# W1's first quarter in two loads: four partitions ahead of everything, the other 124 in the old place

## The chip, the cores and the metric

The kernel runs on one core of one Trainium2 chip. The metric is the device time of one execution in microseconds. Before the change, three executions took 302.37, 302.70 and 302.79 us, a median of 302.7.

## What is computed

Two stages, the second fed by the first. The first is attention with a sliding window: 8 batches, 8 heads, 576 positions, 64 features a head; each position sees the 32 positions on either side of it. The second takes the result as 4608 tokens of 512 features, multiplies it with `w_in` (512 x 2048), takes the square of the positive part, and multiplies with `w_out` (2048 x 512).

```python
scores = scale * np.matmul(q, k.transpose(0, 1, 3, 2))
mask = np.abs(pos[:, None] - pos[None, :]) <= window      # window = 32
...
attn = attn / (np.sum(attn, axis=-1, keepdims=True) + 1e-09)
...
x = np.ascontiguousarray(attn_out.transpose(0, 2, 1, 3)).reshape(B * S, H * D)
h = x @ w_in
r = np.maximum(h, 0.0)
return ((r * r) @ w_out)
```

## The kernel before

The tokens are worked off in 24 groups of 192, three to a batch. For a group, Q and K come into SBUF with positions on the partitions and are turned, so that features lie on the partitions: for the first two batches by TensorE (`turn_pe`, L455 to L500), later by DMA transposes (`turn_dma`, L502). `scores` (L517) multiplies two windows of 128 keys with their queries (L548), ScalarE takes the exponential, VectorE multiplies with the mask (in group 0 a bias does that, L531), and `pv` (L581) multiplies with V, which has a column of ones beside it for the sums (L605). VectorE divides; the result is turned once more (`xturn`, L635) into `XT`, features on partitions, the operand of the second stage.

There `mm1` (L708) multiplies `XT` with 128 columns of W1 at a time, four matmuls that add up over the 512 features (L720). ScalarE takes the positive part (L726), VectorE squares it (L729), and `mm2` (L733) multiplies with W2, four of its sixteen slices at a time (L740).

W1 stands in SBUF as 128 partitions x 4 x 2048 in bf16; in HBM it is float32. It is loaded in four quarters of 512 columns: `load_w1` (L437) issues one DMA a quarter from GpSimd, 128 partitions with 4 rows of 512 elements each, which changes the type on the way. `mm1` waits for the quarter that holds its columns. W2 is loaded in four quarters likewise (L442).

The order of the work is a planner's. Every operation is recorded with its engine, what it reads and writes, a key and an estimated duration; a DMA also has an estimated number of moves and the time of one (`move`). `schedule` (L115) lets each engine take the ready operation with the lowest key, with a model of the DMA queues in it, and `emit` (L220) writes every engine's operations in the planned order, with waits on semaphores: one per engine and one per kind of DMA. Within an engine the order is fixed from then on.

Loads at the start follow a list written by hand, OPENING (L59): entry n gets the key -100 + n. It begins with K of group 1, W1's first quarter, V of groups 0 and 1, Q of group 1. Those are all GpSimd DMAs. Q and K of group 0 do not go through GpSimd but come from SyncE (`load_hw`, L381). Where TensorE would have nothing to do in the first 40 us of the plan, `schedule` puts matmuls on zeros (L207 to L217, issued at L310), called fillers below.

```python
OPENING = [("k", 1), ("w1", 0), ("v", 0, 0), ("v", 1, 1), ("q", 1), ("v", 0, 1), ("q", 2), ("k", 2), ("v", 1, 0), ("w1", 1),
```

Of the kernel before, what the change touches and what calls it, by code (L numbers as in the profile page):

```python
# [18 lines left out]
RING = 1536  # L19
NV, NRAW = 6, 6  # L20
NTURN = 2
NXT = 3
LEAD = 13.0
LAG = 9.0
AHEAD = 9.0
FAR, GFAR = 9.0, 99
TISS = 1340
TMOVE = 15
NVR = 24
# [2 lines left out]
XSLACK = 2500  # L32
LSLACK = 5000
# [5 lines left out]
NPR = 3  # L39
# [5 lines left out]
XTD = 1  # L45
# [222 lines left out]
class Gen:  # L268
# [100 lines left out]
    def load_qk(self, t, b, g, key):  # L369
        t0, n = KC[g] if t == "k" else (192 * g, 192)  # L370
        h = n // 2
        G = 3 * b + g
        raw = self.RAW[t][G % NRAW]
        src = (self.q if t == "q" else self.k)[b]
        s = src[:, t0:t0 + n, :].rearrange("h (j p) d -> p j h d", j=2)
        for j in range(2):
            self.p.rec("POOL", lambda e, j=j: e.dma_start(raw[0:h, j, :].rearrange("p (h d) -> p h d", h=8), s[:, j]),  # L377
                       writes=[("raw", t, G % NRAW, j)], dma=(f"{t}{G % NRAW}{j}", G), key=key, dur=500 + 3 * h,
                       move=(h // 2, 14.5), name=f"{t}{b}{g}{j}", after=self.moe if b > 1 else None, slack=LSLACK if b > 1 else 0)

    def load_hw(self, t, g, key):  # L381

        t0, n = KC[g] if t == "k" else (192 * g, 192)
        h = n // 2
        raw = self.RAW[t][g % NRAW]
        u = 2 * (t == "q")
        f = self.OEB[:, u:u + 2, :].rearrange("p a c -> p (a c)")
        s = (self.q if t == "q" else self.k)[0][:, t0:t0 + n, :].rearrange("h (p r) d -> p h (r d)", r=2)
        oe = [("oe", u), ("oe", u + 1)]
        self.p.rec(HWQ[t], lambda e: e.dma_start(f[0:h, :].rearrange("p (h c) -> p h c", c=128), s), writes=oe,  # L390
                   dma=(f"h{u}", g), key=key, dur=420, move=(h // 2, 27), name=f"h{t}{g}")
        for r in range(2):
            x = f[0:h, :].rearrange("p (h r d) -> p h r d", r=2, d=64)[:, :, r, :]
            y = raw[0:h, r, :].rearrange("p (h d) -> p h d", d=64)
            w = [("raw", t, g % NRAW, r)]
            if HWC[t][r] == "ACT":
                self.p.rec("ACT", lambda e, x=x, y=y: e.activation(y, x, ACTF.Copy), reads=oe, writes=w, key=key, dur=600,
                           name=f"c{t}{g}{r}")
            else:
                self.p.rec("DVE", lambda e, x=x, y=y: e.tensor_copy(y, x), reads=oe, writes=w, key=key, dur=430, name=f"c{t}{g}{r}")  # L400

    def load_pair(self, t, b, g, key):

        t0, n = KC[g] if t == "k" else (192 * g, 192)
        h = n // 2
        G = 3 * b + g
        pr, raw = self.PR[t][G % NPR], self.RAW[t][G % NRAW]
        s = (self.q if t == "q" else self.k)[b][:, t0:t0 + n, :].rearrange("h (p r) d -> p h (r d)", r=2)
        self.p.rec("POOL", lambda e: e.dma_start(pr[0:h, :].rearrange("p (h c) -> p h c", c=128), s), writes=[("pr", t, G % NPR)],  # L409
                   dma=(f"{t}p{G % NPR}", G), key=key, dur=500 + 3 * h, move=(h // 2, 20), name=f"{t}{b}{g}",  # L410
                   slack=LSLACK1 if b else 0)
        self.p.rec("DVE", lambda e: e.tensor_copy(raw[0:h, :, :].rearrange("p r (h d) -> p r h d", d=64),
                                                  pr[0:h, :].rearrange("p (h r d) -> p r h d", r=2, d=64)),
                   reads=[("pr", t, G % NPR)], writes=[("raw", t, G % NRAW, x) for x in range(2)], key=3 * G - LEAD - PKEY if b == 0 else key, dur=430,
                   name=f"c{t}{b}{g}")

    def load_v(self, b, g, key, js=(0, 1)):
        G = 3 * b + g
        vt = self.V[G % NV]
        for j in js:  # L420
            k0 = 192 * g - 32 + 128 * j
            lo, hi = max(k0, 0), min(k0 + 128, S_)
            if g and j == 0 and G < NVR:
                lo = k0 + 64
            n = hi - lo
            self.p.rec("POOL", lambda e, j=j, lo=lo, hi=hi, k0=k0: e.dma_start(  # L426
                vt[lo - k0:hi - k0, j, :, 0:64], self.v[b, :, lo:hi, :].rearrange("h p d -> p h d")),
                writes=[("v", G % NV, j)], dma=(f"v{G % NV}{j}", G), key=key, dur=500 + 3 * n, move=(n // 2, 14.5),
                name=f"v{b}{g}{j}", after=self.moe if b > 1 else None, slack=LSLACK if b > 1 else LSLACK1 * b)

    def copy_v(self, G, key):
# [4 lines left out]

    def load_w1(self, d, key):  # L437
        src = self.w_in[:, 512 * d:512 * d + 512].rearrange("(f p) c -> p f c", p=128)
        self.p.rec("POOL", lambda e: e.dma_start(self.W1[:, :, 512 * d:512 * d + 512], src),  # L439
                   writes=[("w1", d)], dma=(f"w1{d}", 0), key=key, dur=770, move=(32, 81), name=f"w1{d}")  # L440

    def load_w2(self, d, key):  # L442
        src = self.w_out[512 * d:512 * d + 512, :].rearrange("(k p) c -> p k c", p=128)
        self.p.rec("POOL", lambda e: e.dma_start(self.W2[:, 4 * d:4 * d + 4, :], src),
                   writes=[("w2", d)], dma=(f"w2{d}", 0), key=key, dur=770, move=(32, 81), name=f"w2{d}")

# [186 lines left out]
    def xturn(self, G):  # L635
        xa, xb = self.XA[G % 3], self.XB[G % 3]
        key = 3 * G - LEAD + 0.5
        r = 192 * G % RING
        wr = [("xt", (3 * G + c) % (RING // 64)) for c in range(3)]
        if G < NXT:  # L640
# [3 lines left out]
            if two and XTD:  # L644
# [7 lines left out]
                def fa(e):  # L652
                    for j in range(4):
# [6 lines left out]
                           name=f"XT{G}0")  # L660
                for x in (1, 2):
# [3 lines left out]
                    src = hts[x // 2][:, 0:256].rearrange("p (j q) -> p j q", j=2)  # L665
                    w = [(t, x) for t in wr[1:]]
                    if x == 1:
                        self.p.rec("ACT", lambda e, dst=dst, src=src: e.activation(dst, src, ACTF.Copy), reads=tag, writes=w, key=key,
                                   dur=act(256), name=f"XT{G}1")
                    else:  # L670
                        self.p.rec("DVE", lambda e, dst=dst, src=src: e.tensor_copy(dst, src), reads=tag, writes=w + wr[1:], key=key,
                                   dur=dve(256), name=f"XT{G}2")
# [16 lines left out]
            if two:  # L689
                for x, (c0, c1) in enumerate(((0, 64), (64, 192))):  # L690
                    self.p.rec("ACT", lambda e, x=x, c0=c0, c1=c1: e.activation(
                        self.XT[:, :, r + c0:r + c1], (ps, pb)[x][:, 0:768].rearrange("p (j q) -> p j q", j=4)[:, :, c0:c1], ACTF.Copy),
                        reads=(bank, bank2)[x], writes=(wr[:1], wr[1:])[x], key=key - 0.01 * (1 - x), dur=act(4 * (c1 - c0)),
                        name=f"XT{G}{x}")
# [3 lines left out]
                       reads=bank, writes=wr, key=key, dur=act(768), name=f"XT{G}")  # L698
            return
        self.p.rec("SP", lambda e: e.dma_start(self.XT[:, :, r:r + 64], xa[64:128, :], transpose=True),  # L700
                   reads=[("xa", G % 3)], writes=wr[:1], dma=(f"xa{G % 3}", G), key=key - 0.3, dur=TISS, move=(16, TMOVE), name=f"T{G}a",
                   slack=XSLACK)
        self.p.rec("SP", lambda e: e.dma_start(self.XT[:, :, r + 64:r + 192], xb[:], transpose=True),
                   reads=[("xb", G % 3)], writes=wr[1:], dma=(f"xb{G % 3}", G), key=key, dur=TISS, move=(32, TMOVE), name=f"T{G}b", slack=XSLACK)

    def mm1(self, t0, n, ds, key):  # L708
        k = self.k1
        self.k1 += 1  # L710
        ht, rt, gt = self.HT[k % 2], self.RT[k % 4], self.GT
        r = t0 % RING
        c = n * len(ds)
        d0 = ds[0]
        steps = [(t0 // 64 + x) % (RING // 64) for x in range(n // 64)]

        def f(e):
            for x, d in enumerate(ds):
                for ft in range(4):
                    mm = e.matmul(ht[:, n * x:n * x + n], self.W1[:, ft, 128 * d:128 * d + 128], self.XT[:, ft, r:r + n],  # L720
                                  start=(ft == 0), stop=(ft == 3))
            return mm

        self.moe = self.p.rec("PE", f, reads=[("xt", s) for s in steps] + [(("xt", s), 1) for s in steps if t0 < 192 and XTD] + [("w1", d0 // 4)], writes=[f"ht{k % 2}"], key=key,
                   dur=4 * len(ds) * max(n / 2.4 + 2.5, 33), name=f"A{t0}.{d0}")
        self.p.rec("ACT", lambda e: e.activation(rt[:, 0:c], ht[:, 0:c], ACTF.Relu), reads=[f"ht{k % 2}"],  # L726
                   writes=[("rt", k % 4)], key=key, dur=act(c), name=f"r{t0}.{d0}")
        rr = rt[:, 0:c].rearrange("p (d t) -> p d t", d=len(ds))
        self.p.rec("DVE", lambda e: e.tensor_tensor(gt[:, d0:d0 + len(ds), r:r + n], rr, rr, ALU.mult),  # L729
                   reads=[("rt", k % 4)], writes=[("gt", s, d) for s in steps for d in ds], key=key, dur=dve(c),  # L730
                   name=f"g{t0}.{d0}")
# [50 lines left out]
    def build(self):  # L782
        p = self.p
# [19 lines left out]
        for n, it in enumerate(self.opening()):  # L803
            kd, a = it[0], it[1:]
# [18 lines left out]
        for G in range(NG):  # L823
# [7 lines left out]
                    key = 3 * G - LEAD - 0.5 if G >= VCS else key  # L831
                    at(key + 0.01, self.copy_v, G, key - VKEY if G >= VCS else key)
            for t in "kq":
                key = 3 * G - LEAD - (0.6 if b < NTURN else 3)
                at(key, self.turn_pe if b < NTURN else self.turn_dma, t, b, g, key)
            for ws in ((0,), (1,)) if G < NSPLIT else ((0, 1),):
                at(3 * G - LEAD + 0.3 * ws[0], self.scores, G, ws)
# [58 lines left out]
```

## Time and profile before

| | |
|---|---|
| median of three executions | 302.7 us |
| the profiled execution | 302.49 us |
| its span, first to last instruction | 300.5 us |
| granted TensorE clock | 1.000 on average |
| GpSimd's DMA queue (q0) | 106016 packets, 17.93 MB, 87.3% of 16 engines' span |
| SyncE's DMA queue (q1) | 49264 packets, 12.14 MB, 29.6% |
| W1's four loads | 512 KB each, median 11.1 us from issue to landing |

The profile is of one execution. Its times are counted from the first instruction; an engine's busy time leaves out the issuing of DMAs by SyncE and ScalarE, waits and branches. In lists by line, "out<-in" names the tiles. A DMA has two times: how long GpSimd is busy with its issue, and how long it takes from the issue until its semaphore is complete, which is called landing here. The semaphore of a DMA of GpSimd goes up in sixteen steps, and the trace holds the time of each. The DMA share of a stretch is the time that packets took, over the core's 16 DMA engines; it is over 1.00 where packets overlap.

### The profile page before, as it was taken

To read this page: it belongs to the slowest core of one execution; us is meant where nothing else is said; L and a number is where in the kernel's file an instruction comes from. 1 tells how busy PE (TensorE), PEld (TensorE's weight loads), DVE (VectorE), ACT (ScalarE), POOL (GpSimd) and SP (SyncE) were. 2 spreads that over 40 slices of the span, in tenths; PEclk is the share of its full clock that TensorE was granted. 3 is DMA by queue.
4 is the path that set the end of the run, shared out by engine and by line. 5 is a ranking of instruction groups with operands and counts; after the bars stand their busy time and mean duration, and the time that the engine had idled before them with its cause. 6 is when DMAs were issued, how large, how long until landed. Compare 5 with 4: busy or idle time off the path is not lost.

```text
span 300.5 us, 6217 instructions
## 1 busy us (share of the span) xinstructions
PE 291.3 (97%) x2394; PEld 171.1 (57%) x2431; DVE 165.8 (55%) x385; ACT 160.5 (53%) x250; POOL 107.4 (36%) x143
## 2 busy tenths in 40 slices
PE   6899999999999999999999999999999999999996
PEld 2588866847677777754444445445445444444445
DVE  6997785727776766654577756556456322222100
ACT  3596834827467656553756566645646343443312
POOL 8993336506653553665155555420000000000000
PEclk9999999999999999999999999999999999999999
DMA  9999999999999999999999999996121200100112
GB/s 170 176 205 184 196 178 171 156 209 130 164 138 174 191 136 182 143 166 198 190 141 157 138 157 139 185 183 142 55 59 39 61 35 35 37 35 36 37 70 105
DMA packets 160636, 39.83 MB, mean 133 GB/s; under 512 B 149984, under 2 KB 156128, under 8 KB 160608
## 3 DMA queue, kind: packets, MB, share of 16 engines
q0 software_dynamic: 106016, 17.93, 87.3%
q1 hardware_dynamic: 49264, 12.14, 29.6%
q10 hardware_dynamic: 5328, 9.37, 9.5%
q8 instruction: 19, 0.31, 0.5%
q14 instruction: 9, 0.07, 0.1%
HBM read 36.70 MB, written 9.44 MB: 154 GB/s over the span
## 4 chain that ended last, share of the span: by engine, by line
PE 88%; DMA 7%; POOL 3%; issue 1%; ACT 1%; POOLq 0%; ACTq 0%
PE ht L720 40%; PE outp L740 39%; DMA w<-in_moe_w_in_dram 5%; PE at L605 4%; PE at L548 3%; DMA xt<-xb 2%; POOL v L426 1%; POOL w L439 1%; PE at L468 1%; POOL qpair L409 1%; PE ht L765 1%; PE outp L765 1%; POOL kpair L409 1%; ACT oe L750 0%; ACT rt L726 0%
## 5 line engine op out<-in xcount | busy, mean ns | idle before, releaser
L720 PE MATMUL ht<-xt,w 128*128 128x256 bf16 (+2 forms) x886 | 142.7, 302 | 1.6 <-DMA w<-in_moe_w_in_dram 0.6
L740 PE MATMUL outp<-w,gt 128*128 128x512 bf16 x535 | 134.3, 379 | 1.4 <-issue 0.2
L726 ACT ACTIVATE rt<-ht 128x512 bf16<-128x512 f32 (+1 forms) x152 | 86.5, 578 | 91.5 <-PE ht L720 88.1
L720 PEld LDWEIGHTS ht<-xt,w 128*128 128x128 bf16 x896 | 81.0, 98 | 44.1 <-DMA w<-in_moe_w_in_dram 1.0
L729 DVE TENSOR_TENSOR gt<-rt 128x512 bf16<-128x512 bf16 (+1 forms) x152 | 61.5, 408 | 64.3 <-ACT rt L726 62.9
L740 PEld LDWEIGHTS outp<-w,gt 128*128 128x128 bf16 x560 | 52.1, 98 | 55.5 <-ACT oe L750 1.0
L377 POOL DMA_DIRECT2D kraw<-in_k_dram x36 | 27.8, 780 | 88.7 <-PE at L548 45.1
L572 ACT ACTIVATE e<-at 128x1024 bf16<-128x1024 f32 x46 | 44.9, 1023 | 10.3 <-PE at L548 10.1
L577 DVE TENSOR_TENSOR pt<-e,mask 128x1024 bf16<-128x1024 bf16 x46 | 31.5, 691 | 24.9 <-ACT e L572 24.7
L426 POOL DMA_DIRECT2D v<-in_v_dram x48 | 38.1, 808 | 0.0
L750 ACT ACTIVATE oe<-outp 128x512 f32<-128x512 f32 x35 | 21.1, 603 | 23.9 <-PE outp L740 23.9
L377 POOL DMA_DIRECT2D qraw<-in_q_dram x36 | 27.7, 778 | 0.0
L605 PEld LDWEIGHTS at<-v,pt 128*128 128x128 bf16 x384 | 18.2, 98 | 9.7 <-issue 1.4
L605 PE MATMUL at<-v,pt 128*128 128x65 bf16 x384 | 20.0, 194 | 0.6 <-ACT pt L569 0.5
L627 DVE TENSOR_TENSOR xa<-at,rs 64x512 bf16<-64x512 f32 x24 | 16.7, 695 | 0.9
L627 DVE TENSOR_TENSOR xb<-at,rs 128x512 bf16<-128x512 f32 x24 | 16.6, 691 | 0.9
L624 DVE RECIPROCAL rs<-at 64x8 f32<-64x8 f32 (+1 forms) x48 | 10.0, 209 | 10.4 <-PE at L605 9.1
L548 PEld LDWEIGHTS at<-qt,kt 64*128 64x128 bf16 x384 | 10.8, 94 | 8.5 <-issue 6.8
L548 PE MATMUL at<-qt,kt 64*128 64x128 bf16 x384 | 15.3, 217 | 0.3
L633 DVE MEMSET at<- 64x520 f32 x23 | 11.3, 492 | 3.6 <-DVE xa L627 2.7
L433 DVE COPY v<-v 64x512 bf16<-64x512 bf16 x16 | 5.5, 341 | 7.2 <-PE ht L720 6.0
L772 DVE COPY oe<-ht 128x128 f32<-128x128 f32 x1 | 0.3, 292 | 14.5 <-PE ht L765 14.5
(67 smaller groups left out, 81.6 us busy)
## 6 DMA issues: line engine op xcount, KB each, us to landing
out_dram<-oe ACTq DMA_DIRECT2D x35, 256.0 KB, 4.4
qraw<-in_q_dram POOLq DMA_DIRECT2D x36, 96.0 KB, 5.7
w<-in_moe_w_in_dram POOLq DMA_DIRECT2D x4, 512.0 KB, 11.1
v<-in_v_dram POOLq DMA_DIRECT2D x16, 128.0 KB, 7.8
w<-in_moe_w_out_dram POOLq DMA_DIRECT2D x4, 512.0 KB, 18.5
v<-in_v_dram POOLq DMA_DIRECT2D x16, 96.0 KB, 7.3
kraw<-in_k_dram POOLq DMA_DIRECT2D x12, 112.0 KB, 4.7
kraw<-in_k_dram POOLq DMA_DIRECT2D x12, 96.0 KB, 5.6
```

The costliest lines, as they stand in the source:

```text
L377: self.p.rec("POOL", lambda e, j=j: e.dma_start(raw[0:h, j, :].rearrange("p (h d) -> p h d", h=8), s[:, j]), writes=[("raw", t, G % NRAW, ...
L426: self.p.rec("POOL", lambda e, j=j, lo=lo, hi=hi, k0=k0: e.dma_start(vt[lo - k0:hi - k0, j, :, 0:64], self.v[b, :, lo:hi, :].rearrange("h ...
L548: mm = e.matmul(sc[:, 512 * par + 128 * j:512 * par + 128 * j + 128], kt[r:r + 64, j, k0:k0 + 128], q, start=G >= NBIAS, stop=True, skip_g ...
L572: self.p.rec("ACT", lambda e, e_=e_, sc=sc: e.activation(e_[:], sc, ACTF.Exp, scale=0.125), reads=tags[w], writes=[("e", n % 2)], key=key, ...
L577: self.p.rec("DVE", lambda e, pt=pt, ee=ee, mb=mb: e.tensor_tensor(pt[:], ee, mb, ALU.mult), reads=[("e", n % 2), ("mask", mi)], writes=[( ...
L605: mm = e.matmul(avp[:, c:c + 65], pt[:, 4 * (h % 2) + h // 2, :], vt[:, w, h, 0:65], start=(w == 0 and y == 0), stop=True, skip_group_chec ...
L627: self.p.rec("DVE", lambda e: e.tensor_tensor(x[r0:128, :].rearrange("p (x y c) -> p x y c", x=2, y=4), av[:, :, :, 0:64], rb, ALU.mult), ...
L720: mm = e.matmul(ht[:, n * x:n * x + n], self.W1[:, ft, 128 * d:128 * d + 128], self.XT[:, ft, r:r + n], start=(ft == 0), stop=(ft == 3))
L726: self.p.rec("ACT", lambda e: e.activation(rt[:, 0:c], ht[:, 0:c], ACTF.Relu), reads=[f"ht{k % 2}"], writes=[("rt", k % 4)], key=key, dur= ...
L729: self.p.rec("DVE", lambda e: e.tensor_tensor(gt[:, d0:d0 + len(ds), r:r + n], rr, rr, ALU.mult), reads=[("rt", k % 4)], writes=[("gt", s, ...
L740: mm = e.matmul(op[:], gt[:, d, r:r + 128], self.W2[:, d, :], start=(d == 0), stop=(d == 15))
L750: self.p.rec("ACT", lambda e: e.activation(oe, op[:], ACTF.Copy), reads=[f"outp{u % 2}"], writes=[("oe", u % 4)], key=key, dur=act(512), n ...
```

## The change

`load_w1` issues the first quarter as two DMAs. The first carries partitions 0 to 3 (16 rows of 512 elements). Its key is -100.5, below every other load's key, so it is GpSimd's first DMA. The second carries partitions 4 to 127 (496 rows) and keeps the key that the whole quarter had. The other three quarters stay as they are. Each part has a semaphore of its own, and the products with W1's first 512 columns wait for both. The remaining lines of the diff give names to constants and keep their values.

```diff
+TINY = 4
+FIRSTKEY = -100.5
...
     def load_w1(self, d, key):
         src = self.w_in[:, 512 * d:512 * d + 512].rearrange("(f p) c -> p f c", p=128)
-        self.p.rec("POOL", lambda e: e.dma_start(self.W1[:, :, 512 * d:512 * d + 512], src),
-                   writes=[("w1", d)], dma=(f"w1{d}", 0), key=key, dur=770, move=(32, 81), name=f"w1{d}")
+        for i, (p0, p1) in enumerate(((0, TINY), (TINY, 128)) if d == 0 and TINY else ((0, 128),)):
+            self.p.rec("POOL", lambda e, p0=p0, p1=p1: e.dma_start(self.W1[p0:p1, :, 512 * d:512 * d + 512], src[p0:p1]),
+                       writes=[("w1", d) if p1 == 128 else "w1first"], dma=(f"w1{d}{i}", 0), key=key if p1 == 128 else FIRSTKEY,
+                       dur=770 if p1 == 128 else 400, move=(max((p1 - p0) // 4, 1), WMOVE), name=f"w1{d}" if p1 == 128 else "w1first")
...
-        self.moe = self.p.rec("PE", f, reads=[("xt", s) for s in steps] + ... + [("w1", d0 // 4)], writes=[f"ht{k % 2}"], key=key,
+        self.moe = self.p.rec("PE", f, reads=[("xt", s) for s in steps] + ... + [("w1", d0 // 4)] + ["w1first"] * (d0 < 4 and TINY > 0), writes=[f"ht{k % 2}"], key=key,
```

In the built programs the orders on TensorE, VectorE, ScalarE and SyncE are the same; GpSimd has the four partitions' DMA ahead of K of group 1, and 124 partitions where 128 were:

```
before                                        after
L313 Iota dif 128x128                         L322 Iota dif 128x128
                                              L449 DMACopy w1 4x4x512
L409 DMACopy kpair1 96x8x128                  L418 DMACopy kpair1 96x8x128
L439 DMACopy w1 128x4x512                     L449 DMACopy w1 124x4x512
L426 DMACopy v0 96x8x64                       L435 DMACopy v0 96x8x64
L426 DMACopy v1 128x8x64                      L435 DMACopy v1 128x8x64
L409 DMACopy qpair1 96x8x128                  L418 DMACopy qpair1 96x8x128
```

## The prediction

> **What bounds the kernel now.** I read the page's head and busy times first, then TensorE's waits, then the chain of waits up to 30 us, then the opening's timeline and its loads.
>
> ```profile
> span 300.5 us, 6217 instructions
> ...
> PE 291.3 (97%) x2394; PEld 171.1 (57%) x2431; DVE 165.8 (55%) x385; ACT 160.5 (53%) x250; POOL 107.4 (36%) x143
> ```
>
> TensorE (PE) is busy for 97% of the span: whatever delays the start of its dense work is added to the end. TensorE's waits from 30 us on:
>
> ```profile
> PE ht L720 <- ACT oe L750: 0.3, 2, 0.2
> PE outp L740 <- issue: 0.2, 1, 0.2
> PE ht L720 <- issue: 0.2, 1, 0.2
> ```
>
> After 30 us it waits 0.7 us in all, none of it for a DMA. There is no slack later in which a late start could be made good. So the opening decides; the chain of waits there, in order of time (start, us, what):
>
> ```profile
> 8.21 0.68 POOL v L426
> 8.89 1.47 POOL w L439 x2
> 10.36 13.73 DMA w<-in_moe_w_in_dram
> 24.09 0.05 issue
> 24.14 1.49 PE ht L720 x16
> ```
>
> The last quarter of W1 is issued at 10.36 and lands at 24.09; TensorE starts on it at 24.14. Before it come GpSimd's issues, back to back. TensorE's own timeline of these 24 us (start, us; idle time before it in brackets):
>
> ```profile
> 1.20 2.74 PE L310 MATMUL outp<-zz 128*128 128x512 bf16 x6 [1.20 <-DVE zz L304]
> ...
> 7.87 1.68 PE L310 MATMUL outp<-zz 128*128 128x512 bf16 x7
> ...
> 10.13 0.51 PE L468 MATMUL outp<-ident,kraw 96*128 96x96 bf16 x8
> 11.19 0.41 PE L605 MATMUL at<-v,pt 128*128 128x65 bf16 x8 [0.54 <-ACT pt L569]
> 11.44 1.46 PE L310 MATMUL outp<-zz 128*128 128x512 bf16 x6
> ...
> 17.19 0.83 PE L720 MATMUL ht<-xt,w 128*128 128x192 bf16 x8
> ...
> 24.14 1.49 PE L720 MATMUL ht<-xt,w 128*128 128x192 bf16 x16 [0.59 <-DMA w<-in_moe_w_in_dram]
> ```
>
> The reader is to see four points: the first product with V (11.19), the first use of the changed quarter (17.19), the wait for the last quarter (0.59 us at 24.14), and the fillers of L310, which take 457 ns each at the start and 240 ns later.
>
> When each load lands is its issue plus its time to landing, asked of the trace one load at a time. In the order of issue: K of group 1 at 7.44, **W1's first quarter 2.31 + 7.3 = 9.63**, V at 10.35 and 11.15, Q at 12.22, V 13.07, Q 14.20, K 15.05, V 15.53, W1's other quarters 19.44, 21.33, 24.09. The queue serves its loads in that order without a pause: what one load takes longer, all behind it land later. GpSimd's timeline and the first quarter's landing:
>
> ```profile
> 1.41 0.91 POOL L409 DMA_DIRECT2D kpair<-in_k_dram  x1 [0.34 <-issue]
> 2.31 0.78 POOL L439 DMA_DIRECT2D w<-in_moe_w_in_dram  x1
> 3.07 1.68 POOL L426 DMA_DIRECT2D v<-in_v_dram  x2
> ```
> ```profile
> DMA to landing us min/median/max: 7.3/7.3/7.3
> ```
>
> **The change, part by part.** The order of instructions on PE, DVE, ACT and SP is the same in both kernels, fillers included; the renamed constants keep their values. GpSimd gets one more DMA (4 partitions x 4 rows of 512) ahead of all others, and the quarter's own DMA, still second among the old ones, carries 124 partitions. The first product with W1 waits for one semaphore more.
>
> *The extra issue.* Its price is not in the trace. Loads cost GpSimd 0.69 us (64 partitions of V) to 0.91 us (128); 16 packets instead of 512 should be at or below the lower: 0 to 0.9 us, taken 0.5. All GpSimd issues move by that. The queue covers it: V's issue ends at 3.86 and its data comes only after 9.63, 5.8 us later. Only K of group 1, first in the queue, is uncovered: its packets start at 5.1 us in the trace, 2.8 after its issue ended. If that start moves with its issue, all loads move by 0.5; if it hangs on the queue's first issue, it comes earlier.
>
> *The wait.* The small load is first in the queue; it lands long before the 124 partitions. Nothing is late by it: 0.
>
> *The 124 partitions.* This is the term that decides. The quarter is 128 x 4 = 512 packets of one row of 512 elements. In the trace its sixteen completion steps, one a DMA engine, lie between 9.09 and 9.63: equal shares, 32 packets each. Every load of this queue has 64, 80, 96, 112 or 128 partitions, all multiples of 16, and the sixteen completions of each of the nine loads ahead of W1's second quarter lie within 0.7 us. So sixteen equal shares of whole partitions fit all that the trace shows. 124 partitions have no sixteen equal shares; the largest number up to 16 that divides them is 4. No load of this kind was run, so I bound: from 31 or 32 packets an engine (any uneven split over all sixteen; price 0), over 124 (four engines with 31 partitions each), to 496 on one. I take **four engines with 124 packets**, since equal shares are all that the rows show.
>
> The price of a packet: 32 of them lie between K's landing at 7.44 and the quarter's at 9.63, 68 ns each; from 19.44 to 24.09 two quarters land, 73 ns each. Ends: the 100 ns that a packet is recorded to take if nothing overlaps (1.27 x 16 engines x 2 us / 397 packets in the row below), and 39 ns (68 x 203 / 350) if the 203 GB/s of that row could rise to the 350 GB/s that the finest slices of the opening reach. I take 73, the later of the two measured rows.
>
> ```profile
> 7.00:9.00 2.00, 1.52 (x14) 0.96 (x15) 1.86 (x7) 1.25 (x2) 2.00 (x4) 1.00 1.27 203
> ```
>
> 124 - 32 = 92 packets more on the four engines, x 73 ns = **6.7 us** (3.6 to 9.2). A load lands when its slowest engine is done, so every later load of the queue lands 6.7 us later although twelve engines are ahead.
>
> The Trainium skill (DMA: Bandwidth & Descriptors, on why a DMA increments its semaphore by 16) states the same divisor: the largest count up to 16 that divides both outermost sizes, 100 partitions giving 10. The same place names an exception for some direct copies that GpSimd issues, which use all sixteen engines with a rounded-up share. By the rule the sum is this one, by the exception the second case below; no run here shows either.
>
> *What TensorE does with it.* The product with V needs V's 10.35 + 6.7 = 17.05 instead of starting at 11.19: 5.9 us late, since V had 0.84 us to spare. Q (copied from 13.03, landed 12.22) had 0.81, the next V 0.95: no more is added there. The last W1 quarter had fifteen of its engines done by 23.4 and one at 24.09; with 6.7 it lands at 30.1 if the late engine is not among the four, 30.8 if it is: 6.0 to 6.7 after today's 24.14. TensorE's chain without the wait of 0.59 would be there at 23.55 + 5.9 = 29.45, so the load binds.
>
> One thing can add to the chain: TensorE stands still from 10.64 to 17.1. Fillers took 457 ns before 4.48 us, where the clock row of the trace starts, and 240 later. If the clock falls in that pause, the six fillers behind the product cost 6 x (457 - 240) = 1.3 us more: 23.55 + 7.2 = 30.75, again 6.6. So 6.0 to 6.7 either way; I take 6.4. The Trainium skill (TensorE: Matmul & The Clock Gate, Part 1) says that an idle window of some 3.4 us halves the clock; by that the chain's 6.6 would hold, and no row of before has such a pause.
>
> *Sum.* The profiled execution took 302.49 us (span 300.5 and 2.0 around it); the three runs have a median of 302.7, 0.2 more. 302.49 + 6.4 = 308.9, and with the 0.2 **309.0**, rounded between the two.
>
> **The rivals.** That both loads stand where the change puts them is seen in the built order, so none of these is a change that is not made.
>
> *Uneven split over all sixteen (not slower).* If the 124 partitions go out in eights with four left over, fifteen engines carry 32 packets as today. It speaks for it that nothing in the trace forbids it, against it that no unequal load is seen. All loads land as before: 302.7. Within it: if K's start moves with its issue, +0.5 on the wait at 24.14, 303.2; if the queue starts earlier or the engine that ends last at 24.09 is the one with half a share (16 packets, 1.2 us), the wait of 0.59 goes: 302.1. It decides from 32 packets on the fullest engine downwards.
>
> *Two engines or one.* 248 or 496 packets: (248 - 32) x 73 ns = 15.8, about 318; with one 34 us, 336. For it: 2 and 1 divide 124 too; against it, sixteen is the largest divisor in all rows, not a small one.
>
> *Four engines, but cheap.* At 39 ns all loads are 3.6 us late, the last quarter 2.9 to 3.6 after 24.14: 305.4 to 306.1. For it: the other twelve engines move smaller packets meanwhile; against it, 68 and 73 ns are what full queues show.
>
> **How the numbers follow.** Four engines 0.82, uneven over sixteen 0.15, two or one 0.03. The cheap packet is part of the 0.82. The range is that of the four-engine case alone: from 302.5 + 2.9 = 305.4 (39 ns) to 302.7 + 9.2 + 0.6 = 312.5 (100 ns, and 0.6 for a clock that stays low longer than the six fillers). It holds nearly all of 0.82; the rest is left out. About 0.2% (0.6 us) is what a measurement of this kernel can tell from no change. Slower by more: 0.82 + 0.03 + 0.03 of the sixteen (K's start late) = 0.88; within 0.08; faster 0.04.
>
> **What would show it.** Right: the 124-partition load takes about 14 us to landing instead of 7.3 (it lands at about 16 to 17); four of its completions are late and twelve early; TensorE idles about 6 us ahead of L605's first eight matmuls, waiting for a DMA of V; nothing changes from 31 us on but the offset; fillers after the pause show whether the clock fell. Wrong: the quarter lands near 9.6 again, or far beyond 17. The forecast fails if the 124 partitions are not cut in equal shares, or if a lone engine is much faster than 73 ns a packet while the others are quiet.

## The result, and the profile after

The changed kernel takes **309.55 us** (median of six executions, 308.47 to 311.46); the kernel before, run beside it, 302.5. The ratio is 1.0231, with a 95% interval of 1.0207 to 1.0255: slower. Medians and ratios leave out an execution more than 1.5% above the fastest of its kernel; there was one, of 316.06 us, among those with the clock kept up. The profiled execution took 308.47 us, span 306.7; against the 302.49 of before that is 6.0 more, in the span 6.2. Head and busy times of the page:

```profile
span 306.7 us, 6219 instructions
...
PE 293.1 (96%) x2394; PEld 172.1 (56%) x2431; DVE 165.0 (54%) x385; ACT 160.5 (52%) x250; POOL 108.3 (35%) x144
```

TensorE has 1.8 us more of busy time and stands still 4.4 us longer. Its waits (us in total, times, longest), the first and the last three:

```profile
PE at L616 <- DMA v<-in_v_dram: 6.6, 1, 6.6
...
PE ht L731 <- ACT oe L761: 0.3, 2, 0.2
PE outp L751 <- issue: 0.2, 1, 0.2
PE ht L731 <- issue: 0.2, 1, 0.2
```

One wait holds everything: 6.6 us for V of group 0, a load that the change does not touch and that stands right behind the 124 partitions in GpSimd's queue. The waits later on are the three of before, to the tenth. The chain of waits goes from the 124 partitions' issue over that V to the product (start, us, what):

```profile
3.02 1.51 POOL w L449
4.53 13.21 DMA v<-in_v_dram
17.73 0.05 issue
17.78 0.62 PE at L616 x8
```

TensorE's timeline, the rows that answer to those of before:

```profile
10.68 0.51 PE L479 MATMUL outp<-ident,kraw 96*128 96x96 bf16 x8
17.78 0.62 PE L616 MATMUL at<-v,pt 128*128 128x65 bf16 x8 [6.59 <-DMA v<-in_v_dram]
18.21 2.59 PE L319 MATMUL outp<-zz 128*128 128x512 bf16 x6
...
24.44 0.83 PE L731 MATMUL ht<-xt,w 128*128 128x192 bf16 x8
...
30.53 1.48 PE L731 MATMUL ht<-xt,w 128*128 128x192 bf16 x16
```

The first product with V is 6.59 us late, the first use of W1 7.25, the last quarter's first use 6.39; from there to the end the offset stays between 6.1 and 6.4. The six fillers behind the product take 2.59 instead of 1.46 us. The issues on GpSimd, and the time to landing of the third of them, the 124 partitions:

```profile
1.48 0.74 POOL L449 DMA_DIRECT2D w<-in_moe_w_in_dram  x1 [0.41 <-issue]
2.22 0.80 POOL L418 DMA_DIRECT2D kpair<-in_k_dram  x1
3.00 1.54 POOL L449 DMA_DIRECT2D w<-in_moe_w_in_dram  x1
```
```profile
DMA to landing us min/median/max: 14.0/14.0/14.0
```

It lands at 3.00 + 14.0 = 17.0 instead of 9.63. In the trace its sixteen completion steps stand in two groups: twelve from 8.65 to 9.4, four from 16.5 to 17.0. From then on every load of the opening shows the same two groups, V of group 0 for one twelve steps up to 10.5 and four from 17.2 to 17.7; at 46 us the two groups are still 4 us apart. How many engines carry a load can also be counted on the page, in the packets of GpSimd's queue. Before, and after:

```profile
q0 software_dynamic: 106016, 17.93, 87.3%
```
```profile
q0 software_dynamic: 107568, 17.94, 92.3%
```

1552 packets more, with no more data: by their sizes in the trace they are packets of 4 bytes, most of them between 6.0 and 7.5 us. Sixteen are the completions of the additional load. The other 1536 are 12 x (124 + 4): each of the twelve engines without a share seems to be given as many empty packets as a full engine has rows, in both parts of the split quarter. The experiments below use this count.

### The profile page after: what moved, and what is told of

Read it like the earlier page. It is cut to its first block, busy times and chain, and to the rows that moved or that the text cites. A ratio compares the mean times of both kernels' runs of the same rounds, so it can differ in the third digit from the quotient of the medians.

```text
span 306.7 us, 6219 instructions
## 1 busy us (share of the span) xinstructions
PE 293.1 (96%) x2394; PEld 172.1 (56%) x2431; DVE 165.0 (54%) x385; ACT 160.5 (52%) x250; POOL 108.3 (35%) x144
## 4 chain that ended last, share of the span: by engine, by line
PE 92%; DMA 4%; POOL 1%; issue 1%; ACT 1%; POOLq 0%; ACTq 0%
PE ht L731 41%; PE outp L751 39%; DMA v<-in_v_dram 4%; PE at L616 4%; PE at L559 4%; PE outp L319 1%; POOL w L449 1%; PE at L479 1%; PE ht L776 1%; PE outp L776 1%; ACT oe L761 0%; ACT qt L507 0%; PE ht L479 0%; POOL kpair L418 0%; PE at L695 0%
## 5 line engine op out<-in xcount | busy, mean ns | idle before, releaser
L386 POOL DMA_DIRECT2D kraw<-in_k_dram x36 | 27.8, 778 | 89.0 <-PE at L559 61.7
L583 ACT ACTIVATE e<-at 128x1024 bf16<-128x1024 f32 x46 | 44.9, 1023 | 10.2 <-PE at L559 9.9
L319 PE MATMUL outp<-zz 128*128 128x512 bf16 x23 | 8.6, 522 | 1.2 <-DVE zz L313 1.2
```

The lines of the kernel that those rows point to most:

```text
L583: self.p.rec("ACT", lambda e, e_=e_, sc=sc: e.activation(e_[:], sc, ACTF.Exp, scale=0.125), reads=tags[w], writes=[("e", n % 2)], key=key, ...
```

## The experiments

In all of them TensorE, VectorE, ScalarE and SyncE have the same order of instructions as the changed kernel, unless said otherwise. The theory is that of the prediction: a load goes out in equal shares of whole partitions on the largest number of engines up to sixteen that divides them, and the fullest engine sets the landing of everything behind. The rivals blame the split itself, or any count that is no multiple of sixteen. Three dots in an edit stand for lines that give the planner its estimates or name a semaphore's tile.

**16 partitions first, 112 in place.**

```diff
-TINY = 4
+TINY = 16
...
```

> The first load carries 16 partitions and the rest 112; the orders of all engines, the extra issue and the extra wait are as in the changed kernel. Theory (equal shares: a load goes out on the largest number of DMA engines up to 16 that divides its partitions, and 124 leaves four): both loads use sixteen engines, 4 and 28 packets each; the rest lands near 9.6 us after the start of the span and the time is that of before, 302.5 within 0.8. Rival (the split itself costs: the extra load at the head of the queue, its issue, the second semaphore): still 308 to 310.

Measured: 302.74 us, ratio 1.0004 (0.9993 to 1.0014). The 112 partitions land 7.1 us after their issue, at 10.0; the queue has 106032 packets, sixteen more than before. The split, its issue and its semaphore cost nothing that can be measured: the rival falls.

**4 first, then 112 and 12.**

```diff
-        for i, (p0, p1) in enumerate(((0, TINY), (TINY, 128)) if d == 0 and TINY else ((0, 128),)):
+        for i, (p0, p1) in enumerate(((0, TINY), (TINY, TINY + 112), (TINY + 112, 128)) if d == 0 and TINY else ((0, 128),)):
...
```

> The first load keeps its 4 partitions; the other 124 go out as 112 and 12 right behind each other, with one issue more. Theory (equal shares): 112 on sixteen engines with 28 packets, 12 on twelve with 4, so no engine has more than 32 beside the first load's 4; 302.5 to 303.3. Rival (four partitions first are what costs): 308 to 310.

Measured: 302.48 us, ratio 1.0004 (0.9992 to 1.0016), with one load more than the changed kernel. The packets fit too: 106112 are 96 more than before, 32 completions and 12 x 4 + 4 x 4 empty ones (four engines for the 4 partitions, twelve for the 12). Four partitions at the head are not what costs.

**6 first, 122 in place.**

```diff
-TINY = 4
+TINY = 6
...
```

> 6 partitions first, 122 in the old place. Theory (equal shares): 122 is 2 x 61, so two engines carry 244 packets each, 120 more than with 124; at the 79 ns a packet that the changed kernel's four engines show, everything behind lands 9.5 us later than there: the rest at about 26 to 27 us, V of group 0 at about 27, the time 318 to 320. Rival (any load that does not divide by 16 costs the same, for a reason of its own such as padding): 308 to 311.

Measured: 320.24 us, ratio 1.0584 (1.0563 to 1.0605); 0.2 more than the 318 to 320 expected, with the 122 partitions at 27.8 instead of 26 to 27. TensorE's wait and the queue, and the time to landing of the 122 partitions:

```profile
PE at L616 <- DMA v<-in_v_dram: 17.1, 1, 17.1
```
```profile
q0 software_dynamic: 109488, 17.95, 85.5%
```
```profile
DMA to landing us min/median/max: 24.8/24.8/24.8
```

Two completion steps are late (27.8), fourteen early (9.8 to 10.6). 3472 packets more than before are 16 + 14 x 244 + 10 x 4: two engines with 244 rows each, and six for the first load. Two partitions less than in the changed kernel cost 10.7 us more; a flat price for any count that sixteen does not divide is excluded.

**8 first, 120 in place.**

```diff
-TINY = 4
+TINY = 8
...
```

> 8 partitions first, 120 in the old place. Theory (largest divisor up to 16): 120 is 15 x 8, so fifteen engines carry 32 packets each, as before the change: 302.5 within 0.8. First rival (only powers of two count, so eight engines with 60 packets): V of group 0 lands near 12.7 us, 304 to 305.5. Second rival (every count that does not divide by 16 falls to four engines or costs alike): 308 to 311.

Measured: 302.68 us, ratio 1.0003 (0.9987 to 1.0019). 120 is no multiple of sixteen, yet nothing is lost: one completion step at 8.75, fifteen from 9.9 to 10.3, and 80 packets more than before (16 + 1 x 32 + 8 x 4). Fifteen engines carry it, so powers of two have no special place.

**A small first load of other data.** The quarter stays whole; ahead of it all, four partitions go into a tile that nothing reads.

```diff
-TINY = 4
+TINY = 0
...
+        if d == 0:
+            self.p.rec("POOL", lambda e: e.dma_start(self.SPARE[0:4], src[0:4]), writes=["spare"], dma=("spare", 0), key=FIRSTKEY, dur=400,
...
```

> The whole first quarter in one load of 128 partitions as before the change, and ahead of all loads one of 4 partitions into a tile that nothing reads: the first part of the change alone, without its wait. Theory (shares): the small load costs four engines 4 packets each and GpSimd one issue of about 0.7 us, both covered: 302.5 within 0.6. Rival (a first load on four engines holds up the queue): 304 or more.

Measured: 302.39 us, ratio 1.0000 (0.9982 to 1.0018). The first part of the change alone is free.

**The 124 partitions row by row.** Four loads of 124 partitions x 512 in place of one of 124 x 4 x 512.

```diff
+            for f in range(4):
+                self.p.rec("POOL", lambda e, f=f: e.dma_start(self.W1[TINY:128, f, 0:512], src[TINY:128, f, :]),
...
```

> 4 partitions first; the 124 go out as four loads of 124 partitions x one row of 512, so that each side of a load counts along the partitions alone. Theory A (the largest divisor decides whatever the shape): four engines again, 31 packets a load, 124 in all: 309 to 311. Theory B (the exception that the Trainium skill, DMA: Bandwidth & Descriptors, names for some direct copies: all sixteen engines with a rounded-up share): 8 packets a load on fifteen engines and 4 on the last, 32 in all: 302.5 to 303.5, three more issues being covered by the queue.

Measured: 302.86 us, ratio 1.0005 (0.9987 to 1.0023). The same 124 partitions, in the same place, now cost nothing: the last row's load lands at 9.9. 128 packets more than before are 64 completions, 12 x 4 of the first load, and 4 x 4: one engine lacks four rows in each of the four loads, as with 8 partitions on fifteen engines and 4 on the last. Theory B holds for this shape, theory A for the load with a second counted dimension. Size is not what separates them: the loads of 4, 6, 8 and 12 partitions have 16 to 48 rows, fewer than the 124 here, and went by the divisor. But this is the only shape without a second counted dimension that was run.

**Another quarter, far from its consumer.** W1 is as before the change; W2's quarter 1 goes out as 4 and 124 partitions.

```diff
-TINY = 4
+TINY = 0
...
+        for p0, p1 in ((0, 4), (4, 128)) if d == 1 else ((0, 128),):
+            self.p.rec("POOL", lambda e, p0=p0, p1=p1: e.dma_start(self.W2[p0:p1, 4 * d:4 * d + 4, :], src[p0:p1]),
...
```

> W1's first quarter is one load again; the first of W2's quarters in the queue (W2's quarter 1, landing 27.7 us, first used at 37.1) goes out as 4 and 124 partitions in its old place. Theory (four engines carry the 124, and all that is behind them in the queue lands 7.2 us late): the quarter itself, at 35, is still in time, but K of group 3 behind it lands near 36 instead of 28.8 and W2's quarter 3 near 51 instead of 43.8, with 0.4 us to spare: 302.5 + 6.8 = 309.3 (308 to 310.5). Rival (what counts is the uneven load's own consumer, which has 9.4 us to spare): 302.5 within 0.8.

Measured: 310.07 us, ratio 1.0229 (1.0192 to 1.0265). The quarter lands at 34.7 and is used at 45; K of group 3 behind it lands at 36.0. TensorE's longest wait, then its timeline from there:

```profile
PE at L481 <- DVE kraw L421: 3.6, 1, 3.6
```
```profile
36.50 0.93 PE L481 MATMUL at<-ident,kraw 112*128 112x112 bf16 x8 [3.62 <-DVE kraw L421]
...
39.15 2.76 PE L733 MATMUL ht<-xt,w 128*128 128x192 bf16 x16
...
42.75 1.50 PE L733 MATMUL ht<-xt,w 128*128 128x192 bf16 x16
```

The size was right, its make-up was not. Of the 8.2 us that the span of the profiled execution (310.50) grew, 3.6 are the wait for K. Another 1.4 are from the opening, ahead of anything that hangs on the edited load: the last quarter of W1 is first used at 25.56 instead of 24.14. There TensorE waited 0.5 us for a VectorE result and 1.2 us for Q's copy, and then had the clock at 0.5 from 15.3 to 18.7 us; whether the edit has to do with that is open. What is left, 3.2, is about what the clock makes: sixteen matmuls take 2.76 us at 39.15 and 1.50 at 42.75, and the clock row stands at 0.5 from 35.8 to 42.6 us, 6.1 us of it after the wait, half of which is 3.1. The other executions took 308.8 to 310.3, with a mean clock of 0.989 against 0.983 in the profiled one. W2's quarter 3 was waited for no more. The rival falls, in all four executions: a load with time to spare makes those late that have none.

**The clock kept up.** The changed kernel with 29 more fillers ahead of the first product with V; TensorE's order is otherwise the same.

```diff
+            if op.name == "P0A":
+                for k in range(NWARM):
...
+                    out.append(w)
```

> The changed kernel with 29 more fillers on zeros right ahead of the first product with V, so that TensorE is at work (29 x 216 ns = 6.3 us) while it waits for V at 17.7 us. Theory (the pause lets the TensorE clock fall, and the clock makes the changed kernel's time vary from 308.5 to 311.5): the granted clock stays 1.0 from then on, the six fillers behind the product take 1.5 us instead of 2.6, the last W1 quarter (30.2) becomes what TensorE waits for, the median falls to about 308.2 and the runs lie within 1 us. The 6 us of late landing remain. Rival (the landings vary, not the clock): median and spread as in the changed kernel, 309.5, and up to 3 us between runs.

Measured: 310.29 us (median of five, 310.13 to 312.28), ratio 1.0266 (1.0239 to 1.0293), where 308.2 was expected: not faster than the changed kernel. The clock part came as expected, with a mean of 1.000 in all five:

```profile
18.51 0.43 PE L624 MATMUL at<-v,pt 128*128 128x65 bf16 x8 [0.45 <-DMA v<-in_v_dram]
18.78 1.46 PE L327 MATMUL outp<-zz 128*128 128x512 bf16 x6
```

From this product to the first use of W1 it is 6.13 us, against 6.66 in the changed kernel and 6.00 before. But V landed at 18.46 here and at 17.73 there, TensorE waited 0.6 us for ScalarE at 32.89, and the profiled execution (312.28) has two waits later on, for tiles that SyncE's DMAs turn:

```profile
PE ht L739 <- DMA xt<-xb: 1.3, 1, 1.3
...
PE ht L739 <- DMA xt<-xa: 1.2, 1, 1.2
```

Such waits stand in some profiles of the kernels that lost nothing too (0.4 us with 16 partitions first, 1.1 with the small load of other data). They do not explain all of it: three executions took 310.1 to 310.3. Whether the fillers make the loads later, or these executions just had them later, stays open. That a kept clock shortens the whole is not shown; and since these five lie 2.1 us apart at a clock of 1.000, something beside the clock spreads them.

**The changed kernel once more.** No edit.

> The changed kernel once more, unchanged, beside the kernel with more fillers on the same chip. Theory: 308.4 to 311.5, a lower mean clock in the longer runs. Rival: a time that does not go with the clock.

Measured: 309.91 us, ratio 1.0241 (1.0221 to 1.0262). In the profiled execution (310.62) the clock is at 0.5 for 10.2 us, in the first one for 6.8; the last quarter's first use comes at 31.74 instead of 30.53, although the quarter landed nearly alike (30.40, 30.22). Of these 1.2 us V's later landing (18.10, 17.73) is 0.4, and the lower clock can make the rest. Another 0.9 of the 2.2 us by which this execution is longer is a wait for a tile that SyncE's DMAs turn:

```profile
PE ht L731 <- DMA xt<-xb: 0.9, 1, 0.9
```

Over the ten executions of both series the mean is 309.3 at a mean clock of 0.989, 309.9 at 0.983, and the one at 0.978 is the longest, 311.46. So the means go with the clock, but executions of the same mean clock lie up to 1.4 us apart, and a part of that is such waits.

**An earlier start of the queue.** One load for the quarter; the iota moved behind GpSimd's first load. Here the planner also moves masks on VectorE and some fillers.

```diff
-IOTA = -1
+IOTA = 0.5
```

> The kernel before the change (one load for the quarter), with the iota moved behind GpSimd's first load, so that the queue's first issue starts at about 0.85 us instead of 1.41; the planner also reorders the masks on VectorE and some fillers. Theory (the queue starts 2.7 us after its first issue ends, whatever the load): first packets near 4.5 us, the last W1 quarter near 23.6, its wait of 0.6 us gone: 302.0 to 302.5, or slower where the later masks hold up the first scores (303 to 304). Rival (the queue starts at a fixed time near 5 us): landings as before and no gain.

Measured: 302.66 us, ratio 0.9990 (0.9975 to 1.0004). The first issue started at 1.31 instead of 1.41 us, so the iota was not what it had waited for, and the question was not put: inconclusive. No version was measurably faster than the kernel before.

## Why the prediction was right

309.0 was forecast, 309.55 measured. The mechanism was right; that the number came so close is in part luck, since one term was too small and another too large. By its steps:

- *What bounds the kernel, and no slack after 30 us*: confirmed; the later waits are the same 0.7 us.
- *The extra issue, 0 to 0.9, taken 0.5 and covered*: it cost GpSimd 0.74 us and the time nothing (small load of other data, 1.0000). K's packets did not start later with their issue: its first (of 256 bytes) came at 5.0 us instead of 5.1. K landed at 8.52 instead of 7.44 all the same, but TensorE did not wait for it.
- *The wait on the second semaphore, 0*: confirmed; the four partitions land at 6.6.
- *Four engines with 124 packets*: confirmed by the completion steps, the packet count, and the series 120, 124, 122 partitions with 32, 124, 244 packets on the fullest engine and 302.7, 309.6, 320.2 us. The reason given, equal shares of whole partitions, holds for this load but not for every one: row by row the same 124 were shared unequally over sixteen. The Trainium skill (DMA: Bandwidth & Descriptors, on why a DMA increments its semaphore by 16) has both, the divisor and the exception, and these runs agree with both; which shapes fall under the exception it does not say, and here it was the loads that count along one dimension alone (one shape, 124 x 512).
- *73 ns a packet, 6.7 us*: too small. (16.99 - 9.63) / 92 is 80 ns, so 7.4 us. The price did not rise; it had been read too low, as the packets below the list show.
- *What TensorE does with it, 6.0 to 6.7*: 6.39, but by the second of the two paths. V was late by 7.4 and the product by 6.6 where 5.9 was forecast. The queue made up for some of that: the last quarter was late by 6.1, landed at 30.22, inside the 30.1 to 30.8, and TensorE did not wait for it, so "the load binds" did not hold. TensorE's chain did. The clock fell, as the prediction allowed: 0.5 from 13.7 to 20.5 us. The fillers took 1.1 us more of the 1.3 allowed, but short waits of before fell away behind them, so that the chain came at 30.53 where 30.75 was worked out: 23.55 + 6.6 + 0.4 in place of 23.55 + 5.9 + 1.3. The two errors cancel to 0.2 us. The Trainium skill (TensorE: Matmul & The Clock Gate, Part 1) says that an idle window of some 3.4 us halves the clock; the wait of 3.6 us in front of K of group 3 agrees, with 6.8 us at half. The 3.4 us at half from 15.3 us on in the same trace do not fit it: TensorE was busy for 1.67 of the 3.41 us before, and no single wait there is over 1.2 us.
- *The rivals*: uneven over sixteen fell for this load (it is what the row-by-row loads do), two engines fell for 124 and came true for 122, the cheap packet fell. The median lies 1.1 us above the profiled execution, which is the fastest of the ten; the sum had allowed 0.2. A clock that is low longer, which the range's upper end had in it, is part of the reason: three of the six executions have a lower mean clock. It is not all, since two with the profile's own 0.989 took 309.14 and 309.72.

In two stretches the packets of 512 bytes and more are the quarter's rows and nothing else: in the changed kernel from 9 to 15 us, in the kernel before from 7 to 9.

```profile
DMA packets 2914, 0.81 MB, mean 135 GB/s; under 512 B 2609, under 2 KB 2914, under 8 KB 2914
```
```profile
DMA packets 473, 0.41 MB, mean 203 GB/s; under 512 B 85, under 2 KB 473, under 8 KB 473
```

2914 - 2609 = 305 rows in 6 us on four engines are 79 ns each; 473 - 85 = 388 rows in 2 us on sixteen are 82. The 68 and 73 ns of the prediction are distances between landings, and the quarter's first row started at 6.2 us, before the landing at 7.44 from which the 68 was counted. With two engines (27.82 - 9.63) / 212 is 86 ns, but there 124 rows went out from 10 to 15 us, 81 ns each; what is over comes from a late start, with only 28 rows between 6 and 9 us.

## What to carry to other kernels

When a load is cut by partitions, look at what the cut leaves: the fullest DMA engine's packets set the landing, and 124 = 4 x 31 puts 3.9 times as many on it as 128 (14.0 us to landing where 112 partitions took 7.1), while 112, 120 and 16 lost nothing. The price falls on the loads behind it in the same queue, so the uneven load's own slack protects nobody. A wait in front of dense TensorE work can cost twice, by itself and by the clock: after waits of 3.6, 6.4 and 6.6 us the clock was still halved for 6.1, 5.3 and 2.7 us.

## What was not expected of the hardware

- Engines without a share were not free for what is behind. The twelve had the 124 partitions' load done at 8.65 to 9.4, against 9.1 to 9.6 before, although they had none of its data; by the count, 12 x 124 empty packets of 4 bytes went to them instead. And the small loads after it took them longer: from V of group 0 (10.5) to K of group 2 (17.2) 6.7 us, before it was 4.7 (10.35 to 15.05). Why was not tried.
- Inside the kernels the stretches at half clock lasted 3.4, 6.8, 10.2 and 20.5 us, all multiples of 3.41, and for the same kernel 6.8 in one execution and 10.2 in another.
- GpSimd's issue of the large W1 loads lasts by the rows of the fullest engine, not by the data: 0.78 us for 128 partitions, 0.82 for 120 (32 rows each), 1.54 for 124 (124 rows), 2.48 for 122 (244 rows), some 8 ns a row. For small loads that is no rule: the four partitions, with 4 rows an engine, took 0.74.

```profile
L449 POOL DMA_DIRECT2D w<-in_moe_w_in_dram x1: 2477/2477/2477, 3.0 to 3.0; - x1
```

The row is that of the 122 partitions (min/median/max in ns, first and last start in us).
